# Carried state of the first three blocks joined in PSUM, and a new issue order, in a recurrence-and-mixer kernel

## The chip, the cores and the metric

The kernel runs on one core of one Trainium2 chip. Its engines are TensorE (PE; its weight loads are listed as PEld), VectorE (DVE), ScalarE (ACT), GpSimd (POOL) and SyncE (SP), which here only issues transfers. Each engine works through its own list of instructions in order; semaphores hold an instruction until what it needs is there. The metric is device time in microseconds of one execution; lower is better. "Before" is the median of three runs.

## The reference

A gated linear recurrence over 768 steps, for 4 batches and 8 heads of 48 channels, and behind it a mixer with two pairs of matrix products:

```python
for t in range(S):                       # per batch and head, S = 768
    state = alpha[t][:, None] * state + outer(k[t], v[t])     # 48 x 48
    y[t] = q[t] @ state
x = y of all heads side by side          # 768 x 384 per batch
h = relu(x.T @ w_tok1) @ w_tok2          # over the 768 positions, 256 hidden
u = x + h.T
out = u + relu(u @ w_ch1) @ w_ch2        # over 384 channels, 1536 hidden
```

Inputs and output are float32; the kernel's products are bfloat16 with float32 sums.

## The kernel before

**Blocks.** The 768 positions of a batch are cut into three blocks of 256, so there are twelve blocks, numbered 0 to 11; blocks 0 to 2 are batch 0. A block loads four tiles of 384 KB (alpha, k, q, v). With cumulative sums of the logarithms of alpha, made by PE from triangular matrices, keys and queries are scaled so that the recurrence becomes plain products: transposes of keys and queries, a key-query product in two halves ("G"), a causal mask on DVE that also copies it out of PSUM (L709), and a product with the values ("y") to which the part from the carried state is added ("ia", "ib"). Blocks 0 to 5 transpose keys and queries on PE; from block 6 on a transposing transfer does it, issued by SP.

**The carried state.** Each block makes key-value products in PSUM ("K", a pair of banks, one per half of the block). The state behind a half is (K + state before) times the decay of that half. The first state of a batch has no predecessor and is made by one multiplication out of PSUM (`sfirst`, L751). Every other state takes two steps: a sum out of PSUM into an SBUF tile `tmp` on DVE (`sadd`, L754), and a multiplication of `tmp` on DVE or POOL (`smul`, L757). The state is kept in bfloat16, 128 x 384.

**The mixer** of a batch follows its three blocks: token products (L791, L796), a sum (L800), a transposition (on PE for batches 0 and 1, L807), then 24 groups of the first channel product (L815), evacuated with a relu by ACT (L786) or DVE (L788), and six rows of the second (L820), evacuated by DVE (L824) and stored.

**What sets the order.** `build` only names the operations and the engines that may run them. The order of issue on every engine, the engine of each operation and the buffer of each value stand as written lists, `ORDER` and `BUFS`, in the source; `Plan.run` takes them as they are. In `ORDER`, `K1t` means operation K of block 1 on PE; the last letter is the engine: t PE, s ACT, v DVE, g POOL, y SP. A load's engine is the one that issues it, so `ld_vt0y` stands in SP's list and `ld_vt0s` would stand in ACT's list among its computations. All 64 input loads of the kernel before are issued by SP; three of the 25 stores are issued by ACT.

**Fillers.** `f1_` and `f3_` entries are one or three products of 512 columns on a tile of zeros (`fill`), written into a bank whose real content comes afterwards. Thirty such products are in the order before; twelve of them stand ahead of PE's first real work.

Keys, queries and alpha of blocks from 3 on are first multiplied pairwise (`P`, `k0a`, `q0r`; L578, L634, L638), since from there on two positions are joined to one; `scaled` (L642) then multiplies keys and queries by the exponentials. `copy` (L686 on ACT, L687 on DVE or POOL) makes casts, evacuations and moves.

Of the kernel before, what the change touches and what calls it, by code (L numbers as in the profile page):

```python
# [95 lines left out]
HD, DT, DCH = 384, 256, 1536  # L96
# [19 lines left out]
def build(g):  # L116
# [12 lines left out]
    def attention(n):  # L129
# [16 lines left out]
        la, E, IE = V("la"), V("E"), V("IE")  # L146
# [26 lines left out]
        wide = n in WIDE  # L173
# [196 lines left out]
mask0_1v P4g f1_G11t x1_0s E3s IE3s evk2v G1_1t sm1_1g trq2t ldw_wt20y mask1_1v lnP4s vs1_1g ib1t ldw_wt21y vb2s k0a3g  # L370
f3_K2t evq2s K2t f3_G02t y1_1t G0_2t cw_wt10s G1_2t ld_kt4y sa0_2v kk3v ia1t ldw_wc10y mask0_2v sm0_2g vs0_2g cw_wt11s
ldw_wc11y y0_1t t1_0_1_0t t1_0_1_1t t1_0_0_0t t1_0_0_1t ld_qt4y ka3g x0_1s ldw_wc12y kb3g ia2t ib2t ldw_wc13y x1_1s
mask1_2v t1_0_1_2t t1_0_0_2t y0_2t vs1_2s q0r3g t1_0_1_3t cw_wt20g t1_0_0_3t vb3s y1_2t x0_2v ldw_wc14y trk3t
ldw_wc15y t1_0_1_4t t1_0_0_4t x1_2v evk3v t1_0_0_5t qq3g t1_0_1_5t vs1_3s vs0_3s cum4t kc3s ht_0_1s ln14s ht_0_0v K3t
cw_wt21s r14s ld_at5y IE4s t2_0_2t E4s ld_vt4y ld_kt5y s0_3v u_0_2v t2_0_1t sa1_3v t2_0_0t t2_0_3t u_0_0v u_0_3v trq3t
t2_0_4t t2_0_5t up_0_1t u_0_1v up_0_0t k0a4g u_0_5v ldw_wc20y evq3s ld_qt5y ldw_wc21y cw_wc10g ut_0_1s kk4g u_0_4v
ut_0_0v G0_3t G1_3t mask1_3v cw_wc11s ldw_wc22y up_0_2t ib3t ka4g q0r4g qq4g c1_0_0_0t c1_0_2_0t ld_at6y y1_3t
c1_0_1_0t ut_0_2s rt_0_0_0v x1_3v mask0_3v rt_0_1_0s ldw_wc24y ldw_wc23y sm1_3g trk4t cw_wc12s c1_0_2_1t c1_0_3_1t
c1_0_0_1t c1_0_1_1t c1_0_4_1t rt_0_2_0v rt_0_3_1s rt_0_1_1v trq4t cw_wc13s rt_0_0_1s rt_0_2_1s cw_wc14g cw_wc15g
rt_0_4_1v c1_0_6_0t c1_0_7_1t ldw_wc25y evq4v c1_0_9_1t y0_3t rt_0_9_1v P5v evk4s rt_0_6_0s x0_3v c1_0_8_1t c1_0_7_0t  # L380
rt_0_7_1s kc4s c1_0_10_1t c1_0_11_1t vb4g kb4g lnP5s rt_0_7_0s k0a5g ln15s ld_vt5y rt_0_10_1v cum5t G1_4t mask1_4v
rt_0_11_1s r15s rt_0_8_1s G0_4t c1_0_4_0t c1_0_3_0t IE5s mask0_4v vs0_4g ld_at7y kk5v c1_0_10_0t c1_0_5_0t c1_0_5_1t
rt_0_4_0s cw_wc20s c1_0_8_0t q0r5v c1_0_9_0t c1_0_6_1t rt_0_3_0s E5s rt_0_8_0s rt_0_5_1s c1_0_11_0t rt_0_5_0s
rt_0_6_1s trk5t qq5v vs1_4v ia4t y0_4t cw_wc21g rt_0_11_0s K4t trq5t evk5v sa0_4v c2_0_1_0t rt_0_9_0s sm0_4v
rt_0_10_0v cw_wc24g sa1_4v P6v ld_at8y sm1_4v kc5v vb5g cw_wc22s c2_0_5_0t c2_0_2_0t evq5s x0_4s cw_wc23s cw_wc25s
lnP6s ld_kt6y c2_0_2_1t c2_0_5_1t t1_1_1_0t G1_5t G0_5t P7g vs1_5g t1_1_1_1t c2_0_1_1t c2_0_1_2t c2_0_5_2t ld_qt6y
c2_0_1_3t c2_0_5_3t vs0_5s mask0_5v ld_at9y ld_vt6y c2_0_2_2t mask1_5v cum6t o_0_1v o_0_5v K5t c2_0_2_3t ia5t y0_5t
ib4t sa0_5v ln16s sm0_5v o_0_2v lnP7s k0a6g y1_4t cum7t t1_1_1_2t t1_1_0_0t x1_4v ib5t E6s y1_5t t1_1_0_1t t1_1_0_2t
x0_5s c2_0_3_0t r16s ln18s t1_1_0_3t x1_5v t1_1_0_4t t1_1_1_3t t1_1_0_5t IE6s t1_1_1_4t q0r6v kk6v t1_1_1_5t c2_0_0_0t
st_0_5y ld_kt7y ht_1_0s ht_1_1s ld_qt7y st_0_1y c2_0_3_1t t2_1_5t vb6s t2_1_0t E7s u_1_5v t2_1_2t t2_1_3t t2_1_4t  # L390
t2_1_1t u_1_2v u_1_3v c2_0_0_1t c2_0_3_2t qq6g ln17s k0a7g c2_0_0_2t u_1_0v c2_0_4_0t up_1_1t u_1_4v c2_0_3_3t u_1_1v
up_1_0t IE7s P8g ut_1_1v dk6y up_1_2t ka6g kb6s ut_1_0s r17s vs0_6s c2_0_4_1t c2_0_0_3t ld_at10y ld_vt7y o_0_3v
ut_1_2v dq6y kk7g dk7y c1_1_10_1t c1_1_9_1t c1_1_1_1t rt_1_10_1v r18s rt_1_1_1s vs1_6g kc6g lnP8s c1_1_2_0t ld_qt8y
P10v o_0_0v K6t vb7s q0r7g c2_0_4_2t cum8t s0_6v sa1_6v P9g c1_1_2_1t c1_1_0_1t c1_1_10_0t c1_1_3_0t qq7g vs1_7g kb7s
ld_vt8y E8s lnP10s rt_1_0_1s rt_1_2_1v rt_1_10_0v ld_kt8y c1_1_4_1t ld_qt9y rt_1_2_0v rt_1_9_1v ka7s vs0_7s sm1_6v
c2_0_4_3t c1_1_7_0t ld_kt9y dq7y c1_1_11_0t ld_vt9y st_0_0y lnP9s IE8s c1_1_8_1t rt_1_4_1s o_0_4v kc7s rt_1_7_0s
c1_1_9_0t cum9t c1_1_11_1t c1_1_1_0t c1_1_0_0t rt_1_8_1s rt_1_11_1s rt_1_1_0s pq6s ln19s q0r8v rt_1_3_0v rt_1_11_0v
rt_1_9_0v c1_1_5_0t qq8g K7t c1_1_5_1t k0a8g rt_1_0_0v rt_1_5_0v c1_1_3_1t rt_1_3_1s rt_1_5_1s c1_1_6_1t c1_1_7_1t
sa0_7v c1_1_4_0t sm0_7v r19s rt_1_7_1s ld_kt10y dq8y sa1_7v c1_1_6_0t rt_1_6_1v IE9s G0_6t G1_6t rt_1_6_0s rt_1_4_0s
kk8g E9s vb8s ln110s vs1_8s pq7s q0r9g ld_qt10y mask0_6v c2_1_4_0t k0a9g c2_1_4_1t dk8y c2_1_1_0t mask1_6v kk9g ib6t  # L400
y0_6t x0_6v c2_1_4_2t c2_1_4_3t sm1_7g y1_6t c2_1_3_0t st_0_4y c1_1_8_0t o_1_4v st_0_2y G0_7t G1_7t vb9s vs0_8s
rt_1_8_0s mask0_7v c2_1_1_1t qq9g c2_1_3_1t pq8s c2_1_3_2t ia7t y0_7t cum10t r110s E10s mask1_7v k0a10v dk9y kc8s dq9y
c2_1_1_2t c2_1_0_0t c2_1_3_3t c2_1_1_3t q0r10v qq10g K8t o_1_3v x1_6v c2_1_0_1t ka9g sa0_8v ib7t o_1_1v sm0_8g IE10s
vs1_9s vs0_9s x0_7s y1_7t ia8t kb9s ld_at11y G0_8t x1_7s mask0_8v G1_8t t1_2_0_0t t1_2_0_1t t1_2_0_2t t1_2_1_0t kk10g
kc9s t1_2_1_1t t1_2_1_2t c2_1_0_2t st_1_1y ld_vt10y y0_8t t1_2_0_3t pq9g mask1_8v K9t t1_2_1_3t s0_9v x0_8s ib8t y1_8t
x1_8s t1_2_0_4t t1_2_1_4t c2_1_2_0t sa1_9v ln111s ka10g dq10y t1_2_0_5t t1_2_1_5t sm1_9g dk10y kb10g P11g ht_2_1s
r111s ht_2_0v lnP11s vb10s G1_9t G0_9t c2_1_2_1t t2_2_5t c2_1_0_3t mask1_9v ib9t ld_kt11y c2_1_2_2t y1_9t t2_2_3t
mask0_9v t2_2_4t u_2_5v u_2_3v cum11t t2_2_0t y0_9t u_2_4v ux_2_1y vs1_10s st_0_3y x1_9s c2_1_2_3t pq10g IE11s E11s
u_2_0v x0_9v o_1_2v c2_1_5_0t vs0_10g G0_10t t2_2_2t c2_1_5_1t c2_1_5_2t t2_2_1t c2_1_5_3t mask0_10v kc10v ia10t K10t
y0_10t c1_2_8_1t u_2_2v u_2_1v c1_2_3_1t c1_2_7_1t sa0_10v rt_2_3_1s rt_2_8_1v c1_2_5_1t rt_2_7_1s o_1_0v x0_10v  # L410
c1_2_4_1t c1_2_6_1t ld_qt11y rt_2_6_1s ux_2_0y ld_vt11y rt_2_4_1v c1_2_0_1t c1_2_2_1t k0a11g c1_2_1_1t kk11g q0r11g
rt_2_0_1s c1_2_5_0t c1_2_2_0t sm0_10g rt_2_5_1v qq11g sa1_10v rt_2_2_1s st_1_3y dk11y vb11g rt_2_1_1s dq11y kc11g
rt_2_2_0s st_1_4y c1_2_8_0t c1_2_9_0t c1_2_4_0t c1_2_3_0t c1_2_10_1t c1_2_9_1t rt_2_8_0v rt_2_5_0v o_1_5v vs1_11v
rt_2_4_0v sm1_10v vs0_11s rt_2_3_0s c1_2_11_0t rt_2_9_0s rt_2_9_1s c1_2_11_1t K11t rt_2_10_1s c1_2_0_0t rt_2_11_0v
pq11g c2_2_5_0t rt_2_0_0s c2_2_5_1t rt_2_11_1v sa0_11v G0_11t G1_11t G1_10t mask0_11v mask1_10v t1_3_1_0t mask1_11v
c2_2_5_2t st_1_0y c2_2_5_3t c2_2_3_0t c2_2_3_1t ib10t y1_10t t1_3_1_1t t1_3_1_2t c2_2_3_2t x1_10v ia11t y0_11t
t1_3_0_0t sm0_11g t1_3_0_1t x0_11s ib11t t1_3_1_3t y1_11t x1_11v o_2_5v t1_3_1_4t c2_2_3_3t o_2_3v t1_3_0_2t t1_3_0_3t
t1_3_0_4t t1_3_0_5t t1_3_1_5t st_2_5y st_1_2y ht_3_1v c1_2_6_0t c1_2_10_0t ht_3_0s c1_2_1_0t t2_3_0t u_3_0v t2_3_1t
# [460 lines left out]
```

## Time and profile before

| | |
|---|---|
| median of three runs | 166.98 us (165.88 to 167.26) |
| the profiled execution's own time | 167.16 us |
| its span | 165.5 us |
| instructions | 4049 |
| PE, DVE, ACT, POOL busy, share of the span | 93%, 69%, 60%, 47% |
| HBM read, written | 25.17 MB, 4.72 MB |
| share of the 16 DMA engines taken by the main queue | 78.9% |

Times are from the start of the span. "Busy" of PE is modelled from the start of each product, since products overlap in the array. A group line gives engine, operation, tiles, shapes and count; then busy time in us and the mean of one in ns; then the engine's idle time just before these instructions and what ended it. In a timeline the bracket holds the idle time and what ended it.

### The profile page before, as it was taken

How to read it: one execution, taken by the hardware profiler on the slowest of the kernel's cores; microseconds unless marked ns; L12 is line 12 of the kernel's file. 1: busy time of each engine (PE TensorE's matmuls, PEld its weight loads, DVE VectorE, ACT ScalarE, POOL GpSimd, SP SyncE). 2: the span in 40 equal slices, each digit the busy share in tenths (PEclk: the TensorE clock that was granted, in tenths of full speed). 3: DMA queues.
4: the chain of work that ended last, by engine and by line, in shares of the span. 5: the costliest groups of instructions: out<-in, count | busy, mean ns of one | idle time of the engine just before them, and what ended most of it. 6: DMA issues, size and time to landing. Idle time of an engine off the chain costs nothing.

```text
span 165.5 us, 4049 instructions
## 1 busy us (share of the span) xinstructions
PE 153.9 (93%) x1599; PEld 97.9 (59%) x1599; DVE 113.5 (69%) x200; ACT 98.7 (60%) x186; POOL 77.4 (47%) x87
## 2 busy tenths in 40 slices
PE   7849799799999999999999999999899999999992
PEld 2425657376667576665666676665566656566660
DVE  4059999698989987667776888985686703544232
ACT  3776699897999765589899965526502304162100
POOL 4055575899643344876689698397320000000000
PEclk9999999999999999999999999999999999999999
DMA  4999999999999799999999999889401362030114
GB/s 126 318 280 307 275 307 347 350 330 303 263 354 366 199 279 284 270 230 280 218 281 168 263 240 155 189 176 238 120 0 51 111 127 95 19 128 0 48 55 182
DMA packets 76322, 34.46 MB, mean 208 GB/s; under 512 B 68112, under 2 KB 76304, under 8 KB 76304
## 3 DMA queue, kind: packets, MB, share of 16 engines
q1 hardware_dynamic: 75872, 33.63, 78.9%
q10 hardware_dynamic: 432, 0.59, 1.0%
q8 instruction: 12, 0.20, 0.5%
q14 instruction: 6, 0.05, 0.1%
HBM read 25.17 MB, written 4.72 MB: 181 GB/s over the span
## 4 chain that ended last, share of the span: by engine, by line
PE 64%; DMA 13%; POOL 6%; SPq 4%; ACT 4%; issue 3%; DVE 2%; POOLq 0%; DVEq 0%
PE ps L820 26%; PE ps L815 20%; PE ps L593 9%; DMA in<-in_v_dram 6%; DMA in<-in_q_dram 5%; PE ps L791 4%; POOL pkq L642 3%; PE ps L796 3%; SPq L534 3%; DMA tpk<-pkq 3%; PE ps L655 1%; POOL in L638 1%; DVE pkk L642 1%; ACT vb L686 1%; PE ps L807 1%
## 5 line engine op out<-in xcount | busy, mean ns | idle before, releaser
L820 PE MATMUL ps<-wc,rt 128*128 128x384 bf16 (+2 forms) x300 | 53.2, 320 | 0.0
L815 PE MATMUL ps<-ut,wc 128*128 128x384 bf16 x288 | 50.9, 326 | 0.1
L786 ACT ACTIVATE rt<-ps 128x384 bf16<-128x384 f32 x59 | 26.9, 493 | 28.0 <-PE ps L815 27.7
L815 PEld LDWEIGHTS <-wc 128*128 128x128 bf16 x288 | 27.4, 98 | 17.7 <-issue 0.4
L820 PEld LDWEIGHTS <-rt 128*128 128x128 bf16 x300 | 27.6, 98 | 16.7
L709 DVE TENSOR_TENSOR gtm<-ps,mk 128x1024 bf16<-128x1024 f32 x24 | 28.5, 1219 | 4.6 <-PE ps L593 3.4
L788 DVE TENSOR_SCALAR rt<-ps 128x384 bf16<-128x384 f32 x37 | 19.4, 553 | 13.3 <-PE ps L815 13.2
L824 DVE TENSOR_TENSOR o<-ps,u 128x384 f32<-128x384 f32 (+2 forms) x25 | 13.1, 536 | 12.9 <-PE ps L820 12.9
L642 POOL TENSOR_TENSOR pkq<-in,E 128x768 bf16<-128x768 f32 x9 | 16.3, 1816 | 5.2 <-DVE in L638 3.3
L642 POOL TENSOR_TENSOR pkk<-in,IE 128x768 bf16<-128x768 f32 x7 | 12.7, 1817 | 9.4 <-ACT E L626 7.5
L686 ACT CAST vb<-in 64x384 bf16<-64x384 f32 (+1 forms) x22 | 14.1, 640 | 3.6 <-DMA in<-in_v_dram 2.3
L800 DVE TENSOR_TENSOR u<-ps,x 128x384 bf16<-128x384 f32 x24 | 12.1, 552 | 3.9 <-PE ps L796 3.6
L593 PE MATMUL ps<-zs 128*128 128x512 bf16 x30 | 9.7, 457 | 2.6 <-ACT IE L626 1.2
L791 PE MATMUL ps<-x,wt 128*128 128x384 bf16 x48 | 11.1, 326 | 0.0
L796 PE MATMUL ps<-ht,wt 128*128 128x384 bf16 x48 | 9.9, 327 | 0.8 <-POOL wt L687 0.8
L634 POOL TENSOR_TENSOR in<-in,in 128x384 f32<-128x384 f32 x8 | 8.0, 999 | 5.7 <-DVE pkk L687 2.6
L686 ACT CAST x<-ps 128x384 bf16<-128x384 f32 x12 | 5.5, 480 | 7.9 <-PE ps L593 7.8
L754 DVE TENSOR_TENSOR tmp<-ps,ss 128x384 f32<-128x384 f32 x16 | 8.8, 553 | 0.7 <-PE ps L593 0.3
L687 POOL CAST vb<-in 64x384 bf16<-64x384 f32 (+1 forms) x12 | 7.0, 581 | 4.8 <-DMA in<-in_v_dram 2.4
L593 PE MATMUL ps<-tpq,tpk 48*64 48x128 bf16 (+1 forms) x288 | 8.2, 219 | 0.8 <-POOL tpq L687 0.7
L757 POOL TENSOR_TENSOR ss<-tmp,E 128x384 bf16<-128x384 f32 x9 | 7.5, 834 | 3.0 <-PE ps L593 1.6
L593 PE MATMUL ps<-vb,gtm 128*128 128x48 bf16 x192 | 8.7, 184 | 0.0
(91 smaller groups left out, 208.2 us busy)
## 6 DMA issues: line engine op xcount, KB each, us to landing
in<-in_alpha_dram SPq DMA_DIRECT2D x12, 384.0 KB, 5.4
in<-in_q_dram SPq DMA_DIRECT2D x12, 384.0 KB, 5.6
in<-in_k_dram SPq DMA_DIRECT2D x12, 384.0 KB, 5.6
in<-in_v_dram SPq DMA_DIRECT2D x12, 384.0 KB, 5.5
in<-in_moe_w_ch_dram SPq DMA_DIRECT2D x12, 384.0 KB, 6.3
out_dram<-o SPq DMA_DIRECT2D x20, 192.0 KB, 2.4
in<-in_moe_w_tok_dram SPq DMA_DIRECT2D x4, 384.0 KB, 5.5
out_dram<-o ACTq DMA_DIRECT2D x3, 192.0 KB, 1.9
```

The costliest lines, as they stand in the source:

```text
L593: return self.pe.matmul(out, lhsT=lhsT, rhs=rhs, start=start, stop=stop, skip_group_check=True)
L642: self.shared(self.eng[e].tensor_tensor(self.t(dst)[:, :, :, 0:D], self.t(src).rearrange("p h s d -> p s h d"), bass.AP(tensor=f.tensor, o ...
L686: return self.act.copy(d, s)
L709: self.nc.vector.tensor_tensor(self.t(gtm)[:, hf, :, :], self.pair(gp).rearrange("p a (j t) -> p (a j) t", t=128), bass.AP(tensor=m.tensor ...
L786: self.act.activation(d, s, AF.Relu)
L788: self.nc.vector.tensor_scalar_max(d, s, 0.0)
L791: self.pe.matmul(self.bank(bank)[:, 0:HD], lhsT=self.wt1[:, kc, m * 128 : m * 128 + 128], rhs=self.t(x), start=(kc == 0), stop=(kc == NS - 1))
L796: self.pe.matmul(self.bank(bank)[:, 0:HD], lhsT=self.wt2[:, kc, i * 128 : i * 128 + 128], rhs=self.t(hts[kc]), start=(kc == 0), stop=(kc = ...
L800: self.nc.vector.tensor_tensor(self.t(u)[:, i % 3], self.bank(bank)[:, 0:HD], self.t(x), ALU.add)
L815: self.pe.matmul(self.bank(bank)[:, 0:HD], lhsT=self.wc1[:, kc, mc * 128 : mc * 128 + 128], rhs=self.t(ut)[:, 3 * half : 3 * half + 3, kc, ...
L820: self.pe.matmul(self.bank(bank)[:, 0 : cz - ca], lhsT=self.t(rts[mc][0])[:, i * 128 : i * 128 + 128], rhs=self.wc2[:, mc, ca:cz], start=( ...
L824: self.nc.vector.tensor_tensor(self.t(o)[:, ca:cz], self.bank(bank)[:, 0 : cz - ca], self.t(u)[:, i % 3, ca:cz], ALU.add)
```

## The change

For blocks 0 to 2, a state that has a predecessor is no longer summed on DVE. The predecessor (bfloat16, in SBUF) is multiplied with the identity on PE and added to the key-value products that lie in the PSUM bank; then one multiplication out of PSUM on DVE, the function that made first states, makes the new state. That holds for four states: the second half of block 0, both halves of block 1, and the first half of block 2. The names `sa` and `sm` stay, on PE and DVE in place of DVE and DVE or POOL. From block 3 on nothing changes in the computation.

```diff
         states = [before]
         for hf in range(nst):
             s_, sp = V("ss"), states[-1]
-            if sp is None:
+            if sp is not None and not turned:
+                ad = O(f"sa{hf}_", pe([384]), 10 + hf, writes=[kp], reads=[sp[0]], preds=[KO, sp[1]],
+                       emit=lambda e, hf=hf, s0=sp[0]: g.sjoin(kp, s0, hf))
+                so = O(f"sm{hf}_", dve(384), 11 + hf, writes=[s_], reads=[kp, E], preds=[ad, et],
+                       emit=lambda e, s_=s_, hf=hf: g.sfirst(s_, kp, E, hf, wide))
+            elif sp is None:
                 so = O(f"s{hf}_", dve(384), 10, writes=[s_], reads=[kp, E], preds=[KO, et],
...
+    def sjoin(self, kp, s0, hf):
+        self.mm(self.bank(kp, hf)[:, 0:HD], self.idn, self.t(s0), False, True)
```

The lists `ORDER` and `BUFS` are replaced as a whole. The head of the old and of the new order:

```diff
-ld_at0y f3_trq0t f3_cumw1t f3_cumw0t f3_G00t ln0s ld_at1y ld_at3y ld_qt0y f1_trk0t cumw0t ld_kt0y ln1s ld_vt0y E0s
-cumw1t ld_vt1y ld_kt1y Et0s ln13s qq0v IE0s ld_at2y IE1s E1s f3_K0t f1_K0t kk0g P3g trq0t trk0t vb0s K0t f1_G00t evq0v
...
+ld_at0y ln0s ld_kt0y ld_vt0s cumw0t ld_at1y ln1s E0s ld_at3s ld_qt0y qq0v ld_kt1y cumw1t IE0s kk0v ld_at2y IE1s kk1g
+trq0t Et0s vb0s f1_trk0t f1_K0t E1s ln2s K0t trk0t ld_qt2s ld_vt1y f1_G00t ld_qt1y f3_G00t Et1s s0_0v evq0v evk0s
+sa1_0t sm1_0v P3v f3_y0t G1_0t ln13s vb1s vs1_0g ld_kt2y G0_0t lnP3s mask1_0v cumw2t trk1t ld_kt3s K1t ldw_wt10s IE2s
```

What the new lists hold, counted against the old ones: 21 of the 64 loads are issued by ACT (ten of them ahead of the first L815 product of batch 0), and 11 of the 25 stores. Fillers are 18 products, none ahead of PE's first real work. Of the query scalings on DVE or POOL (`qq`), six are on POOL in place of nine, that of block 11 among those now on DVE. In the pair of steps that scale block 3's queries, `q0r3` is now on DVE and `qq3` stays on POOL; `cw_wt20`, a cast of a token weight, moves from POOL to DVE, and `cw_wt21` stays on ACT. `kk1` and `kk3` move from DVE to POOL and `kk0` from POOL to DVE; `evk0`, the copy of block 0's transposed keys, moves from DVE to ACT. The relu evacuations stand at 57 on ACT and 39 on DVE in place of 59 and 37; the evacuations of `x` at 18 and 6 in place of 12 and 12. The transfers that transpose stay on SP; `ld_vt11`, on SP ahead of the two transposes of block 11 before, is on ACT.

More of the change, by code (lines that the diff above doesn't have):

```diff
@@ L370 @@
[L370 to L404, printed above, removed]
@@ L415 @@
[L415 to L418, printed above, removed]
-c1_2_7_0t t2_3_2t st_2_3y u_3_1v t2_3_5t c2_2_4_0t rt_2_7_0v u_3_2v t2_3_3t rt_2_1_0s rt_2_6_0s c2_2_1_0t t2_3_4t
@@ new lines @@
+rt_3_10_1s rt_3_4_0v rt_3_9_1v c2_3_1_0t c2_3_2_0t c1_3_8_1t rt_3_9_0v c1_3_3_1t rt_3_1_1v rt_3_8_1v rt_3_3_1v
+rt_3_4_1s c2_3_4_0t c2_3_3_0t c2_3_1_1t c2_3_5_0t c2_3_0h1_0t c2_3_1_2t c2_3_3_1t st_2_0s rt_3_11_0s rt_3_10_0v
+c2_3_0h1_1t c2_3_0h1_2t c2_3_5_1t c2_3_0h1_3t c2_3_4_1t c2_3_1_3t c2_3_4_2t c2_3_4_3t c2_3_0h0_0t c2_3_2_1t c2_3_2_2t
+c2_3_3_2t o_3_1v o_3_0h1v st_2_1s c2_3_5_2t o_3_4v st_3_4s c2_3_2_3t c2_3_5_3t o_3_5v c2_3_3_3t c2_3_0h0_1t st_3_1y
+o_3_3v c2_3_0h0_2t o_3_2v st_3_5s st_3_0h1y c2_3_0h0_3t st_3_3y o_3_0h0v st_3_0h0y st_3_2s
```

81 lines of the change are left out of this document (57 added, 24 removed), and 22 rows, old and new, of the table BUFS.

## Prediction

> **What bounds the kernel now.** I read the page first, then busy time in chosen stretches, then the chain of waits through the places where the TensorE was not full.
>
> ```profile
> span 165.5 us, 4049 instructions
> PE 153.9 (93%) x1599; PEld 97.9 (59%) x1599; DVE 113.5 (69%) x200; ACT 98.7 (60%) x186; POOL 77.4 (47%) x87
> ```
>
> The share of PE is modelled and says little by itself. Stretches say more. The columns are: stretch, its length, busy time of PE, PEld, DVE, ACT and POOL with instructions begun, granted clock, DMA share, GB/s.
>
> ```profile
> 1.06:4.90 3.84, 3.84 (x10) 1.36 (x11) 1.83 (x17) 1.49 (x2) 1.59 (x7) 1.00 0.75 200
> 12.80:30.20 17.40, 15.22 (x246) 10.37 (x242) 17.25 (x23) 14.34 (x25) 9.93 (x14) 1.00 1.09 313
> 36.50:162.20 125.70, 124.58 (x1233) 79.60 (x1229) 86.71 (x147) 71.00 (x142) 56.66 (x56) 1.00 0.75 186
> ...
> sum 30.00, PE 23.93 PEld 15.60 DVE 22.83 ACT 24.33 POOL 17.27; mean PE 3.99 PEld 2.60 DVE 3.81 ACT 4.06 POOL 2.88
> ```
>
> The last line sums the six stretches from 5 to 35 us. The reader is to see three regimes. From 36.5 to 162.2 us PE is busy 124.58 of 125.70 us: there the kernel costs its matrix products and nothing else, and no product in that part is added or taken away. Before 36.5 us no engine rules alone: from 12.8 to 30.2 us DVE is busy 17.25 of 17.40 us, and the DMA share is 1.09, so the transfers are full too. ACT has 30.00 - 24.33 = 5.67 us free between 5 and 35 us. So the change can be worth what it does to the start of the long PE stretch, plus the few holes inside it (125.70 - 124.58 = 1.1 us by this view).
>
> How the start comes about is in the chain of waits (start, length, what):
>
> ```profile
> 21.99 7.64 DMA in<-in_q_dram
> ...
> 29.77 0.99 POOL in L638
> ...
> 30.76 0.82 POOL wt L687
> 31.59 1.79 POOL pkq L642
> ...
> 33.42 0.63 PE ps L655 x8
> ...
> 34.08 1.34 ACT tpq L686
> ...
> 35.45 0.62 PE ps L593 x16
> 36.08 0.44 PE ps L807 x6
> 36.52 0.17 PE ps L593 x4
> 36.69 0.33 PE ps L815 x2
> ```
>
> The queries of block 3 land at 29.63 us; POOL scales them, casts a weight piece in between, scales again; PE transposes, ACT copies out, and after products and a transposition the first channel product (L815) runs at 36.69 us. It is no matter of blocks 0 to 2 at all.
>
> **The change part by part.** The state, by groups:
>
> ```profile
> L754 DVE TENSOR_TENSOR tmp<-ps,ss 128x384 f32<-128x384 f32 x16 | 8.8, 553 | 0.7 <-PE ps L593 0.3
> L757 POOL TENSOR_TENSOR ss<-tmp,E 128x384 bf16<-128x384 f32 x9 | 7.5, 834 | 3.0 <-PE ps L593 1.6 <-DVE pkk L642 1.2
> L751 DVE TENSOR_TENSOR ss<-ps,E 128x384 bf16<-128x384 f32 x4 | 2.2, 550 | 0.4 <-PE ps L593 0.4
> L593 PE MATMUL ps<-la,u 128*128 128x384 bf16 x18 | 4.9, 325 | 0.5 <-ACT rt L786 0.3 <-ACT la L587 0.2
> ```
>
> Four sums of 0.553 us leave DVE (2.2 us), three of the four products after them leave POOL (2.5 us) and come to DVE at 0.550 (1.65 us). Four identity products of 384 columns come to PE; none stands in the trace, and the nearest row is L593 la,u, 0.325 us each to the end. One step of the state falls from 0.553 + 0.834 to 0.325 + 0.550 us, half a microsecond, four times. On the path to 36.69 us this is worth nothing directly, since that path runs through block 3. Off it, DVE's own list up to block 0's first token evacuation stays about as long (a weight cast, a query scaling and two multiplications of keys or alpha come to it, two key scalings and two copies out leave it). The join also adds a wait: an identity product stands in PE's queue until the state before it is made, with fillers, the other mask products and the next block's transposes behind it. In the start PE has idle time for that: the two rows below are idle times of 1.54 and 1.05 us. If the cover went, it would cost at most a step's 0.55 us four times.
>
> ```profile
> 12.13 0.62 PE L655 MATMUL ps<-idn,pkk 128*128 128x128 bf16 x8 [1.54 <-POOL pkk L642]
> 18.86 0.62 PE L655 MATMUL ps<-idn,pkq 128*128 128x128 bf16 x8 [1.05 <-POOL pkq L642]
> ```
>
> *Order at the start.* In the new order the query scaling of block 3 (0.99 us on POOL) is on DVE, where the same form takes about the L751 time, 0.55, and the weight cast (0.82 us) is no longer between it and POOL's second scaling. With the landing where it is, the chain shortens by 0.44 + 0.82 = 1.26 us. But the copy on ACT at 34.08 us has its own predecessors, and these do not move: the second piece of the second token weight is cast there first.
>
> ```profile
> 31.88 0.83 ACT L686 CAST wt<-in 128x768 bf16<-128x768 f32 x1 [0.56 <-DMA in<-in_moe_w_tok_dram]
> ```
>
> In both orders a logarithm-sized operation and two exponentials of some 0.45 us follow before the copy; from 32.7 that is 33.9 to 34.1 us, so with this landing only 0.2 us are won. In the new order that piece is issued on ACT ahead of the loads for block 4, so it may land about one transfer sooner. The ends are thus 0.2 and 1.26 us earlier; I take 0.9, nearer the chain that the profile names.
>
> *Loads on ACT.* Ten loads move to ACT's queue before the first channel product, and some twenty in all. What an issue costs there:
>
> ```profile
> 0.81 2.39 SPq L534 DMA_DIRECT2D in<-in_alpha_dram  x3
> 3.24 1.15 SPq L534 DMA_DIRECT2D in<-in_q_dram  x1
> ...
> L534 SPq DMA_DIRECT2D in<-in_alpha_dram x5: 455/1077/1262, 0.8 to 15.2; - x5
> ...
> L574 ACTq DMA_DIRECT2D out_dram<-o x3: 338/377/444, 156.6 to 161.0; - x3
> ```
>
> The third and fourth rows give shortest, median and longest ns. An issue is 0.455 us when the queue is empty and 1.1 us behind others; ACT's few stores at the end took 0.377. With 0.46 the ten cost 4.6 us. Counted by the two orders up to the third copy of the transposed mixer input, ACT also loses three casts of 0.83 us and gains one copy out of PSUM; three operations of some half a microsecond leave and three come.
>
> ```profile
> L686 ACT COPY tpk<-ps 128x1024 bf16<-128x1024 bf16 x1 | 1.0, 1023 | 0.0
> ```
>
> That is 3 x 0.83 - 1.02 = 1.5 us less. So 3.1 us must fit into its 5.67 free ones, and they do, with 2.6 us over. I cost the loads at nothing; the cover is gone when an issue takes over (5.67 + 1.5)/10 = 0.72 us.
>
> By the Trainium skill (DMA: Bandwidth & Descriptors, "Issuing engines are not separate DMA queues") DMAs from any engine run on the same 16 engines and interleave, and a second issuing engine saves only issue time. The share of 1.09 agrees; by that rule nothing lands sooner, which is the second rival below.
>
> *Fillers.* Before, 30 products of 512 columns on zeros keep PE occupied; afterwards 18, none of them ahead of the first real work. The first stretch above shows ten starts in 3.84 us, 0.43 us each; later three take 0.66 us until the next group, 0.22 each:
>
> ```profile
> 24.20 0.82 PE L593 MATMUL ps<-zs 128*128 128x512 bf16 x3
> 24.86 0.36 PE L593 MATMUL ps<-vb,gtm 128*128 128x48 bf16 x8
> ```
>
> So PE begins at half rate although the granted clock reads 1.00, and the fillers took that phase. Now the first cumulative products (four of 384 columns for each of two blocks) will. Eight products of 384 columns take about 8 x 0.16 = 1.3 us more so (384/512 of the 0.22 us at full rate is 0.16), among waits for loads; I cost it at nothing, at most 1.3.
>
> *Block 11.* The one clear hole in the long stretch:
>
> ```profile
> 111.89 1.81 POOL L642 TENSOR_TENSOR pkq<-in,E 128x768 bf16<-128x768 f32 x1
> 113.73 1.23 SPq L666 DMA_TRANSPOSE tpk<-pkq  x1
> 118.71 1.32 POOL L687 COPY tpq<-tpk 128x1024 bf16<-128x1024 bf16 x1 [2.57 <-DMA tpk<-pkq]
> 120.09 0.86 PE L593 MATMUL ps<-tpq,tpk 48*64 48x128 bf16 x48 [0.67 <-POOL tpq L687]
> L642 DVE TENSOR_TENSOR pkq<-in,E 128x768 bf16<-128x768 f32 x3 | 2.9, 956 | 5.7 <-DMA in<-in_q_dram 5.6
> ```
>
> POOL's 1.81 us scaling releases the transposing transfer, then POOL's copy, then PE, 0.67 us late. The new order gives the scaling to DVE (0.956), and block 11's values load on ACT's queue rather than ahead of the transposes on SP. It stands 0.85 us earlier, the hole closes: -0.7. The transfer could land no sooner behind other traffic: then 0.
>
> *All else* (eight more stores on ACT, evacuations dealt out anew among ACT and DVE, which are busy 71.00 and 86.71 us of the 125.70) lies beside a full PE: 0, between -0.4 and some +4 us.
>
> **Sum.** 167.16 us for the profiled execution (span 165.5 and 1.66 around it) - 0.9 - 0.7 = 165.6. The median of the runs shown is 166.98, so 0.8% under it. One per cent, 1.67 us, is about what a measurement of this kernel can tell from no change; the main case lies from 164.0 to 166.6.
>
> **Rivals.**
> *Holes close beyond that.* ACT and PE in the middle:
>
> ```profile
> 75.00:80.00 5.00, 4.56 (x32) 2.55 (x30) 4.31 (x9) 4.25 (x11) 3.19 (x3) 1.00 1.07 276
> ```
>
> 0.44 us is idle there, behind a knot of ACT work that the new order spreads; with the full 1.26 at the start it gives 167.16 - 1.26 - 0.7 - 0.44 = 164.8, and with an earlier landing of one load (1.1 us) 163.7. Take 164.2. Against: every order leaves knots of its own.
>
> *Transfers rule.* The same bytes through full queues: the last needed weight lands at 31.88 as now, 0.2 gained, block 11 waits for its transfer: 167.0. For it: the share of 1.09; against: the chain through POOL.
>
> *The change is slow to wake PE.* With half rate reaching into blocks 0 and 1, 1.3 us and a like sum for transposes, half covered: 165.6 + 1.3 = 166.9. By the Trainium skill (TensorE: Matmul & The Clock Gate, "What's actually happening") the array leaves half rate only after some 3.4 us of sustained work; the ten slow starts agree, and the figure says nothing about scattered work.
>
> *ACT's queue blocks* (slower). If a load on ACT waits for room as SP's do, at 1.15 us, ten cost 11.5 us; less 1.5 and the free 5.67 leaves 4.3 us on the path to the first channel product: 167.16 + 4.3 - 0.7 = 170.8. It decides from 0.72 us an issue on. For it: SP's median 1.077, and ACT waits in order, so a load held for a buffer holds the evacuations behind it. Against: only a third load in a row was slow at the start, and ACT's stand apart.
>
> *New holes* (slower). The order of every engine is new over 125 us that are now full to 1.1 us; three or four holes like block 11's put 3 us on: 168.9 and more.
>
> **How the numbers follow.** Main case 0.36 (somewhat over a third of it under 165.3), closing holes 0.17, transfers 0.08, waking 0.04, ACT's queue 0.20, new holes 0.15. Faster by over 1% (under 165.3): 0.13 + 0.17 = 0.30. Slower by over 1% (over 168.65): 0.20 + 0.15 = 0.35. Within: 0.23 + 0.08 + 0.04 = 0.35. The range reaches from 163.6 to 170.8 and leaves out some 0.04 below and, of the last two rivals, the worse halves. That the join does not take place is no case of its own: 16 sums would still stand on DVE, at the same time within 0.5 us.
>
> **What would show it.** The first L815 group before 36 us; rows of identity products on the state of 0.33 us and 12 sums left at L754; ACT's load issues near 0.46 us (wrong if near 1.1, with idle DVE and PE behind them); no wait of PE for the query copy of block 11; PE busy over 124 us in the 125 before its last product. I am wrong if the first L815 comes after 37 us or PE's waits for ACT grow by microseconds.

## The result and the profile after

The changed kernel takes 168.53 us in the median of four executions against 166.43 us for the kernel before on the same chip; the ratio is 1.011, with a 95% interval of 1.0062 to 1.0158. Beside later kernels it was run once more, at 1.0158 (1.009 to 1.0227). It is slower by a little over one per cent, and the forecast said 0.8% faster. Ratios and intervals, here and below, are of undisturbed executions alone, while medians are of all; in three runs below (the new run of the changed kernel, the join in the old order, and the first kernel with both the load on SP and zero products at the front) the profiled execution was a disturbed one, and of their traces only one wait of the first is used.

The profiled execution of the changed kernel took 167.97 us. The head of its page, with the granted clock in 40 slices:

```profile
span 166.3 us, 4027 instructions
PE 153.1 (92%) x1591; PEld 98.4 (59%) x1591; DVE 118.1 (71%) x205; ACT 96.3 (58%) x185; POOL 67.9 (41%) x79
PEclk9999995999999999999999999999999999999998
```

There is something new in the third line: in the seventh slice, 25 to 29 us, TensorE had half its clock. In the kernel before all forty slices read 9.

The stretches of the changed kernel (stretch, length, busy time of PE, PEld, DVE, ACT, POOL, granted clock, DMA share, GB/s), from two questions:

```profile
20.00:25.00 5.00, 2.96 (x49) 2.25 (x47) 3.24 (x4) 2.55 (x6) 2.28 (x3) 1.00 1.14 338
25.00:30.00 5.00, 5.00 (x80) 3.75 (x78) 3.51 (x5) 3.85 (x7) 4.08 (x5) 0.66 1.10 359
...
38.10:162.90 124.80, 124.56 (x1233) 79.52 (x1232) 92.05 (x152) 69.57 (x142) 48.67 (x51) 1.00 0.71 175
```

PE is busy 2.96 of the 5 us from 20 us on, then 5.00 of 5, but at a mean clock of 0.66. The long stretch is fuller than before: 0.24 us of it are idle (124.80 - 124.56) in place of 1.12. The first kind of its channel products, with the first and the last start, by the view of that line:

```profile
L822 PE MATMUL ps<-ut,wc x288: 322/326/337, 38.1 to 151.9; 128*128 128x384 bf16 x144
```

It starts at 38.08 us against 36.52 us in the timeline of the kernel before (36.69 us is where the chain of waits comes to it): 1.56 us later. From there to the start of the kernel's last product it is 124.58 us (38.08 to 162.66) against 125.36 us (36.52 to 161.88): 0.78 us shorter. 1.56 - 0.78 = 0.78 us is the difference of the two profiled executions (167.97 - 167.16 = 0.81). The ratio of 1.011 is more than that, 1.8 us; the hybrid orders below bear on why.

What ends at 38.10 us, in the chain of waits of the changed kernel (start, length, what):

```profile
21.30 1.43 SPq L560
22.73 0.05 issue
22.78 8.86 DMA in<-in_k_dram
31.64 0.02 issue
31.66 0.37 ACTq L560
32.03 0.04 issue
32.07 0.52 ACT pkk L690
32.59 0.05 issue
32.64 0.79 PE ps L597 x14
33.43 1.01 PE ps L803 x6
...
38.10 0.95 PE ps L822 x5
```

The chain no longer runs through block 3's queries. SP's load of block 4's keys lands at 31.64 us; 0.02 us later **ACT issues a load** (`ldw_wc15`, a piece of an output weight), and only then comes ACT's copy `pkk` of block 3's keys, for which the key-value products wait. Block 4's keys are used by neither the copy nor the issued load. The landings in the trace raise eight semaphores in turn, whichever engine issued the load; the record of this load's instruction names the semaphore that it waits for, and it is the one that block 4's keys raised last. ACT's list stands at the load until then. So a wait for a transfer of SP's stands in ACT's list, and ACT's computations behind it. The timeline has the same, and an earlier stall (start, length, what, and in brackets the idle time before and what ended it):

```profile
22.78 0.86 SPq L538 DMA_DIRECT2D in<-in_k_dram  x1
24.60 0.50 PE L597 MATMUL ps<-vb,pkk 64*128 64x96 bf16 x8 [1.99 <-POOL vb L691]
28.16 0.73 PE L798 MATMUL ps<-x,wt 128*128 128x384 bf16 x2
31.66 0.37 ACTq L560 DMA_DIRECT2D in<-in_moe_w_ch_dram  x1
32.64 0.34 PE L597 MATMUL ps<-vb,pkk 128*128 128x96 bf16 x4 [0.92 <-ACT pkk L690]
```

At 24.60 us PE has waited 1.99 us for POOL's cast of block 2's values. The half clock follows that stall. Two causes offered themselves, then: ACT held by a load's wait, and stalls of PE with what they do to the clock.

### The profile page after: what moved, and what is told of

Read it like the earlier page. It is cut to its first block, busy times and chain, and to the rows that moved or that the text cites. A ratio compares the mean times of both kernels' runs of the same rounds, so it can differ in the third digit from the quotient of the medians.

```text
span 166.3 us, 4027 instructions
## 1 busy us (share of the span) xinstructions
PE 153.1 (92%) x1591; PEld 98.4 (59%) x1591; DVE 118.1 (71%) x205; ACT 96.3 (58%) x185; POOL 67.9 (41%) x79
## 4 chain that ended last, share of the span: by engine, by line
PE 79%; DMA 8%; DVE 6%; SPq 3%; ACT 1%; issue 1%; ACTq 0%; DVEq 0%
PE ps L822 28%; PE ps L827 27%; PE ps L597 13%; DMA in<-in_k_dram 5%; PE ps L803 4%; PE ps L798 4%; DMA in<-in_alpha_dram 3%; DVE gtm L713 2%; PE ps L659 2%; PE ps L814 1%; DVE u L807 1%; SPq L560 1%; SPq L538 1%; DVE pkk L646 1%; SPq L554 1%
## 5 line engine op out<-in xcount | busy, mean ns | idle before, releaser
L827 PE MATMUL ps<-wc,rt 128*128 128x384 bf16 (+2 forms) x300 | 54.1, 320 | 0.0
L793 ACT ACTIVATE rt<-ps 128x384 bf16<-128x384 f32 x57 | 25.8, 489 | 23.8 <-PE ps L822 21.9
L795 DVE TENSOR_SCALAR rt<-ps 128x384 bf16<-128x384 f32 x39 | 20.2, 552 | 11.0 <-PE ps L822 9.8
L690 ACT CAST x<-ps 128x384 bf16<-128x384 f32 x18 | 8.6, 479 | 10.1 <-PE ps L597 8.6
L646 POOL TENSOR_TENSOR pkq<-in,E 128x768 bf16<-128x768 f32 x6 | 10.9, 1815 | 7.7 <-DVE wt L691 3.0
L597 PE MATMUL ps<-la,u 128*128 128x384 bf16 x18 | 5.8, 388 | 6.0 <-ACT la L591 6.0
L798 PE MATMUL ps<-x,wt 128*128 128x384 bf16 x48 | 11.1, 331 | 0.0
L646 DVE TENSOR_TENSOR pkq<-in,E 128x768 bf16<-128x768 f32 x6 | 5.7, 955 | 6.1 <-ACT E L630 5.0
L582 POOL TENSOR_TENSOR in<-in 128x384 f32<-128x384 f32 x6 | 6.0, 999 | 8.0 <-DVE wc L691 3.9
L597 PEld LDWEIGHTS <-gtm 128*128 128x128 bf16 x192 | 7.9, 98 | 2.3 <-issue 1.0
L691 POOL CAST vb<-in 64x384 bf16<-64x384 f32 (+1 forms) x10 | 5.3, 533 | 7.9 <-ACT vb L690 5.3
```

The lines of the kernel that those rows point to most:

```text
L597: return self.pe.matmul(out, lhsT=lhsT, rhs=rhs, start=start, stop=stop, skip_group_check=True)
L646: self.shared(self.eng[e].tensor_tensor(self.t(dst)[:, :, :, 0:D], self.t(src).rearrange("p h s d -> p s h d"), bass.AP(tensor=f.tensor, o ...
L690: return self.act.copy(d, s)
L793: self.act.activation(d, s, AF.Relu)
L795: self.nc.vector.tensor_scalar_max(d, s, 0.0)
L798: self.pe.matmul(self.bank(bank)[:, 0:HD], lhsT=self.wt1[:, kc, m * 128 : m * 128 + 128], rhs=self.t(x), start=(kc == 0), stop=(kc == NS - 1))
```

## Experiments

**The two parts of the change, apart.** The join in the old order, and the new order without the join.

```diff
 (old order, join: sa on PE, sm on VectorE directly behind it)
-sa1_0v
+sa1_0t sm1_0v
...
 (new order, no join)
-sa1_0t sm1_0v
+sa1_0v sm1_0v
```

One of the four states is shown; the other three are changed alike.

> The kernel before, with its order, and only the join: four sums on PE instead of DVE, the multiplication behind each out of PSUM on DVE right behind it. If the loss comes from the new order: same time as before within 0.5% (0.997 to 1.003), first L815/L822 product at 36.0 to 36.9 us. Rival 'the join itself costs' (PE holds its queue for the state before): PE waits of 0.3 us or more in front of identity products and a first channel product at 37.5 us or later, ratio 1.008 or more.

> The changed kernel, with its order, but the old computation of the state: the four sums on DVE, the multiplications on DVE behind them. Theory 'new order': the stall at block 2's products and the late start stay, ratio 1.009 to 1.016, with up to 0.5 us more since DVE does 1.9 us more work in a stretch in which it is full only up to 23.5 us. Rival 'the join costs': ratio falls to 1.003 or less.

Measured: the join in the old order 167.41 us, ratio 1.0056 (1.0034 to 1.0078); the new order without the join 169.99 us, 1.0185 (1.0126 to 1.0244). The first lies between the two ranges that were expected, the second above its range. So most of the loss is the order's, not the join's. The join costs half a per cent in the old order; in the new order it is worth some 0.7% by the midpoints (1.0185 against 1.011), with intervals that overlap and on two chips. Without it PE waits longer, for POOL's copy of values of block 0, and POOL's copy has waited 1.31 us for the state's multiplication on DVE. In the source that multiplication (`smul`) goes through `shared`, which makes such operations of DVE and POOL follow each other in order of issue; the join's multiplication (`sfirst`) does not.

```profile
19.89 0.32 PE L592 MATMUL ps<-vb,gtm 128*128 128x48 bf16 x4 [2.33 <-POOL vb L686]
```

**Block 2's values earlier.** Loaded ahead of block 4's alpha, and cast on POOL ahead of block 4's pairwise product.

```diff
-ld_kt2y ... ld_at4y ... ld_vt2y ... P4g ... vb2g
+ld_kt2y ld_vt2y ... ld_at4y ... vb2g P4g ...
```

> The changed kernel, with the load of block 2's values issued ahead of block 4's alpha, and POOL's cast of them ahead of POOL's product for block 4. Theory 'late values' (PE stood 2.0 us at block 2's key-value products because these values landed at 23.6 us, behind loads that ACT had issued): the values land near 21 us, that wait falls under 0.5 us, the granted clock between 25 and 30 us stays at 1.00, the first L822 product comes at 36.5 to 37.0 us instead of 38.1, and the kernel at 0.995 to 1.003 of the kernel before. Rival 'ACT is held' (an issue on ACT waits for a load of SP): the wait before K of block 3 at 31.4 us stays at about 1 us, the first L822 product comes no more than 0.5 us sooner, ratio 1.007 to 1.011. Rival 'cold start': no difference over 0.3 us, ratio 1.011.

Measured: 168.57 us, 1.0108 (1.0072 to 1.0143): no gain. The stall at 24.6 us goes and the first x product (L798) stands at 25.3 us in place of 28.2, but PE then waits before block 3's keys, and runs at half rate after it:

```profile
28.23 0.62 PE L659 MATMUL ps<-idn,pkk 128*128 128x128 bf16 x8 [1.53 <-POOL pkk L646]
...
29.31 1.13 PE L798 MATMUL ps<-x,wt 128*128 128x384 bf16 x3
```

Three products of 384 columns take 1.13 us here, some 0.32 us from one start to the next, against 0.16 at full rate. The first channel product stays at 38.12 us, as the rival "ACT is held" had it: the stall was beside the chain that ended last, and ACT's wait (1.55 us idle before the copy) still ended it.

**The output weight's load off ACT, or later on ACT.** In the first kernel SP issues it; in the second it stays on ACT, behind the two casts it held.

```diff
-cw_wt20v ldw_wc15s kc3s
+cw_wt20v ldw_wc15y kc3s
...
-ldw_wc15s kc3s t1_0_1_5t ht_0_0v K3t cum4t ht_0_1s qq3g
+kc3s t1_0_1_5t ht_0_0v K3t cum4t ht_0_1s ldw_wc15s qq3g
```

> The changed kernel, with one load, the last piece of the first channel weight, issued by SP instead of ACT at the same place of the order. Theory 'ACT is held': ACT's move of block 3's keys comes at about 31.2 instead of 32.07 us, PE's wait before block 3's products falls from 0.9 to about 0, the first L822 product comes about 0.9 us sooner (37.2 us), ratio about 1.005. Theory 'late values': the stall of 2.0 us at 22 to 24.6 us stays as it is, and of the 1.6 us by which the first L822 product is late at least 0.7 stay. If only the late values mattered, the first L822 product would stay at 38.1 us.

> The changed kernel with one move on ScalarE's queue: the load of the sixth output-weight tile is issued behind the scaled-key cast and the first hidden-state cast (ht) instead of ahead of them; it stays on ScalarE. Theory 'ScalarE is held by the load's wait': the casts no longer stand behind a wait that ended only when a transfer of SyncE's queue landed, so the time comes out as in the run that gave this load to SyncE, whose first y product stood at 37.2 us and whose ratio was 1.0035: first y product at 37.0 to 37.4 us, 167.2 to 167.6 us. Rival 'SyncE's queue': what helped there was the changed order of SyncE's issues and landings; then the first y product stays at 38.1 us and the time at 168.4 to 168.6 us.

Measured: on SP 167.41 us, 1.0035 (1.000 to 1.007); later on ACT 167.35 us, 1.0076 (1.0034 to 1.0119). In neither trace does PE wait before block 3's key-value products. ACT's copy and these products in the second:

```profile
29.85 0.50 ACT L690 COPY pkk<-pkk 64x384 bf16<-64x384 bf16 x1
30.41 0.34 PE L597 MATMUL ps<-vb,pkk 128*128 128x96 bf16 x4
```

The first channel product stands at 37.2 and 36.7 us in place of 38.1, as the wait's theory said, though the two profiled executions are not quite of one kind with the changed kernel's. Both have a whole clock (1.00), where most of the others of the same kernels read 0.979 to 0.990. In the first the whole start ran some 2.7 us later (the identity product of block 1's second half at 20.24 us in place of 17.54), so that the stall at 24.6 us could not arise; in the second that stall was 1.25 us. By times the first is decided: beside it on the same chip stands the kernel with block 2's values first, which keeps the load at its old place, at 1.0108 (1.0072 to 1.0143). The times of the second were run on another chip, and its interval reaches that of the changed kernel, so by times alone it is not decided; the kernels with zero products in the stall, below, decide it.

**Zero products put back at the front.** Nine of them, where PE stands still until 5.2 us; then the same with the load on SP, and then with block 2's values first as well.

```diff
-ld_at0y ln0s
+ld_at0y f3_trq0t f3_cumw1t f3_cumw0t ln0s
```

> The changed kernel with nine zero products of the kernel before put back ahead of the first cumulative product, where TensorE otherwise stands still until 5.2 us. Theory 'cold start': the products between 5.2 and 11 us, spaced 0.32 us apart in the changed kernel, run at 0.16 us, block 0's gate arrives some 0.5 us earlier and about half of that or more reaches the first y product: 37.4 to 37.8 us, 167.8 to 168.2 us. Rival 'the start is covered': loads land in turn at 1.2 us apart, and the phase ends with what the late loads and ScalarE allow; then the first y product stays within 0.2 us of 38.1 and the time within 0.3 us of 168.5.

> Both edits at once: the sixth output-weight tile loaded by SyncE (0.9 us by its own run) and the nine zero products at the front. If each cost is a term of its own: 166.6 to 167.2 us, first y product at 36.4 to 36.9 us. If the start is covered: 167.2 to 167.6 us, as with SyncE's load alone, first y product at 37.2 us. If the earlier start only lets TensorE run into the wait for block 2's values (2.2 us in the changed kernel, not seen in the run with SyncE's load): a hole of 1 us or more stands before block 2's key-value products again, and the time is 167.4 us or more.

> The two edits and the third, block 2's values loaded ahead of block 4's gate inputs and cast ahead of block 4's mask product on GpSimd. Alone this third edit changed the time by nothing (1.0108) because the hole came back before block 3's keys. Theory 'ScalarE and the start were the bound': with them gone the values count, first y product at 36.0 to 36.5 us and 166.0 to 166.6 us. Rival 'holes wander': the wait comes back elsewhere between 20 and 32 us and the time is that of the two edits, or longer.

Measured: 169.68 us, 1.0185 (1.009 to 1.028); 167.0 us, 1.0063 (1.0017 to 1.011); 166.6 us, 1.004 (1.0004 to 1.0075). The first came out worse than both of its theories, with the first channel product at 39.5 us. The cold start is not shown to cost this change anything. With the zero products ahead of them the first real products still run at half rate, but the second group, block 1's, runs at full rate, where the changed kernel still has half rate (its row last):

```profile
3.59 1.49 PE L597 MATMUL ps<-zs 128*128 128x512 bf16 x3
5.15 1.12 PE L597 MATMUL ps<-la,u 128*128 128x384 bf16 x3
7.59 0.65 PE L597 MATMUL ps<-la,u 128*128 128x384 bf16 x3 [0.77 <-ACT la L591]
...
7.63 1.12 PE L597 MATMUL ps<-la,u 128*128 128x384 bf16 x3 [0.74 <-ACT la L591]
```

So the half rate does end sooner, but the groups start when ACT has made the logarithms of alpha, at 5.2 and 7.6 us with the zero products or without, and what they win there is not in the time. The first kernel stalls for ACT's copy later, longer than the changed one did:

```profile
32.93 0.34 PE L597 MATMUL ps<-vb,pkk 128*128 128x96 bf16 x4 [2.15 <-ACT pkk L690]
```

The second is no faster than the load on SP alone (1.0035, on another chip). What the third gains over the second, 0.2%, is within their intervals. Its time reaches the range of the first theory of its expectation (166.0 to 166.6 us), but not by that theory: its first channel product stands at 37.3 us and not at 36.0 to 36.5, behind a stall of 1.53 us before block 3's keys, at half rate again, as the rival "holes wander" had it.

**Keeping PE busy through the stall.** Seven zero products in the stall before block 2's key-value products; alone, and with the load behind ACT's casts. A third kernel has the late load, block 2's values first, and the seven zero products in the stall that this leaves before block 3's keys. The changed kernel was run beside them.

```diff
-E3s IE3s K2t
+E3s IE3s f3_K2t f1_K2t f3_y1t K2t
...
-y0_2t ... trk3t
+y0_2t ... f3_trk3t f1_trk3t f3_y2t trk3t
```

> The changed kernel once more, unaltered, so that the runs beside it share a chip with it: 168.0 to 169.0 us, ratio 1.007 to 1.016, mean granted clock 0.986 to 0.990, first y product at 37.9 to 38.3 us.

> The changed kernel with seven zero products ahead of block 2's key-value products, in the hole of 2.2 us in which TensorE waits for block 2's values. They end before the values come, so no product of the kernel is later. Theory 'the hole lowers the clock': no half-rate products follow at 25 to 28 us, the mean granted clock comes back to 0.996 or above in nearly all executions, and the first x products come 0.5 to 1.2 us earlier; as ScalarE's scaled-key cast still ends at 32.6 us the first y product gains only 0.2 to 0.6 us: 167.9 to 168.3 us. Rival 'the clock is no matter of the hole': clock 0.987 again and 168.5 us. Third: if ScalarE's wait alone binds, the clock is whole and the time is still 168.5 us.

> The same seven zero products, and the load of the sixth output-weight tile issued behind ScalarE's two casts (alone 1.0076 and a clock of 0.986 to 0.99 in most executions). If the two costs add up: clock 0.996 or above, first y product at 36.4 to 36.8 us, 166.3 to 166.9 us, ratio 1.000 to 1.004. If the clock is no matter of the hole: as without the zero products, 167.3 us or ratio 1.007.

> The late load, block 2's values loaded and cast first (its hole gone, but one of 1.7 us then stands before block 3's keys), and seven zero products in that hole. If all three costs of the new order are then paid back and its gain in the long stretch (0.8 us) stays: clock 0.996 or above, first y product at 35.8 to 36.4 us, 165.4 to 166.2 us, ratio 0.994 to 1.000. Rival 'the landings rule the first phase': first y product at 36.7 us or later and a ratio of 1.003 or more, whatever is warm.

Measured, on one chip: the changed kernel 169.1 us, 1.0158 (1.009 to 1.0227); zero products alone 169.15 us, 1.0185 (1.012 to 1.025); with the late load 166.48 us, 1.0039 (1.0007 to 1.0072); with the values first too 166.38 us, 1.0029 (0.9995 to 1.0063).

No theory had the zero products alone right: the half rate at 25 us goes, PE is earlier, and runs into ACT's wait that much harder. The timeline of that kernel:

```profile
31.58 0.37 ACTq L560 DMA_DIRECT2D in<-in_moe_w_ch_dram  x1
31.99 0.51 ACT L690 COPY pkk<-pkk 64x384 bf16<-64x384 bf16 x1 [2.00 <-DMA in<-in_k_dram]
32.56 0.34 PE L597 MATMUL ps<-vb,pkk 128*128 128x96 bf16 x4 [1.99 <-ACT pkk L690]
...
33.41 2.72 PE L803 MATMUL ps<-ht,wt 128*128 128x384 bf16 x8
```

ACT's idle time ahead of the copy is 2.00 us, PE's is 1.99, and now the half clock comes after this stall: eight products of 384 columns in 2.72 us, 0.32 us apart. The window says so too:

```profile
33.40:37.60 4.20, 4.20 (x34) 2.59 (x32) 2.73 (x7) 2.37 (x5) 4.12 (x5) 0.65 1.12 341
```

So ACT's wait hid the stall: with the stall removed alone, the wait stalls PE for 2 us in its place and halves its clock for some 3 us more. With the load late as well (timeline of the kernel with the late load and the zero products):

```profile
29.99 0.51 ACT L690 COPY pkk<-pkk 64x384 bf16<-64x384 bf16 x1
30.55 0.34 PE L597 MATMUL ps<-vb,pkk 128*128 128x96 bf16 x4
31.68 0.38 ACTq L560 DMA_DIRECT2D in<-in_moe_w_ch_dram  x1
32.09 0.83 ACT L690 CAST wt<-in 128x768 bf16<-128x768 f32 x1 [0.91 <-DMA in<-in_k_dram]
32.98 0.50 PE L803 MATMUL ps<-ht,wt 128*128 128x384 bf16 x2 [0.38 <-ACT wt L690]
```

The copy is made at 29.99 us, two microseconds sooner, and the wait, still there, holds a later cast for 0.91 us and PE for 0.38. By the chain of waits the first channel product, at 36.4 us, still comes behind that cast. The granted clock, 0.979 to 0.990 in the eight executions of the changed kernel, is 0.997 to 1.000 in all ten of this one, and in all ten of the next. The time comes back from 1.0158 to 1.0039, as the expectation "the two costs add up" had it; the next, at 1.0029 with its first channel product at 36.6 us, lies between its two theories.

The wait's share is shown: the kernel with zero products alone and this one differ by the place of one load, on one chip, and stand at 1.0185 (1.012 to 1.025) and 1.0039 (1.0007 to 1.0072). The share of the stall and of the lowered clock is not. Among the executions of the late load alone, three with a clock of 0.997 or more took 166.6 to 167.1 us (166.86 in the middle), and the other six that its ratio counts 167.45 us in the median; that makes some 0.6 us, as an estimate. But between kernels it does not show: with the late load, zero products or none are 1.0039 against 1.0076 on two chips; the load on SP alone gave 1.0035 with a clock of 0.986 to 0.990 in eight of ten executions, and the kernel with SP's load, zero products at the front and the values first 1.004 with 0.976 to 0.990 in all ten.

**What is left of the gain.** The old order for its first 302 entries (up to block 4's key-value products) and the new one from there; and the old order for 612 entries, so that of the change only block 11's part and what follows it is left.

```diff
 ORDER:
-the new order from its first entry
+302 (or 612) entries of the old order, then the new order's remaining entries
 (state sums of blocks 0 to 2 on VectorE; 15, or 8, values in another buffer of their kind)
```

> The order of the kernel before up to and with the key-value products of block 4 (302 entries, state sums on VectorE, all loads on SyncE there), and from there the new order; a dozen values take another buffer of their kind so that lifetimes do not meet. If the first phase is the whole loss and the long stretch's gain of 0.8 us (the closed hole of block 11 and a shorter stall near 76 us) is real: ratio 0.995 to 0.997, first y product within 0.3 us of the kernel before. If the gain lies beside the path that ends last, or comes only with the new first phase: ratio 0.999 to 1.003. If the seam makes holes of its own: above 1.003, with holes right behind 50 us.

> The order of the kernel before for 612 entries (to some 100 us), and from there the new order: of the change only block 11's part (its query scaling on VectorE, its value load on ScalarE, the stores) is left. If the hole of block 11 was worth its 0.7 us: ratio 0.995 to 0.997 and no TensorE wait for block 11's transposed queries. If the wait goes and the time stays, it was made up for later: ratio 0.999 to 1.002.

Measured: 167.29 us, 1.0058 (1.0031 to 1.0085), and 166.2 us, 1.0009 (0.9982 to 1.0035). The first has a hole behind its seam:

```profile
53.11 0.83 ACT L686 CAST wc<-in 128x768 bf16<-128x768 f32 x1 [2.02 <-DMA in<-in_moe_w_ch_dram]
...
53.66 1.14 PE L823 MATMUL ps<-wc,rt 128*128 128x384 bf16 x6 [1.99 <-DVE tmp L757]
```

It is not of the kind of the changed kernel's: ACT waits for the weight that it casts, and PE for DVE's sum of a state. So this hybrid says little on the gain. The second has no such hole, and block 11's queries come in time:

```profile
117.57 0.65 PE L823 MATMUL ps<-wc,rt 128*128 128x384 bf16 x3
118.15 0.86 PE L593 MATMUL ps<-tpq,tpk 48*64 48x128 bf16 x48
```

There is no wait in brackets where the kernel before had 0.67 us. Still the stretch from the first channel product to the last product is 125.36 us long, the same as before, and the time is the same. In the ten profiles used here that have the new order from start to end, this stretch was between 124.5 and 125.3 us: 0.1 to 0.9 us shorter. Of the kernel before there is one profile, so how far its own stretch varies is not known.

Both hybrids also show something about the kernel before. Their first 302 entries are its own, and their first channel products stand at 34.9 and 35.1 us, 1.6 and 1.4 us ahead of the profiled execution that the forecast started from. A difference shows where transfers were slower in that execution (a window of the second hybrid, and from its timeline the wait for block 0's keys):

```profile
10.00:15.00 5.00, 4.40 (x70) 2.56 (x69) 3.82 (x6) 4.79 (x9) 2.98 (x3) 1.00 1.17 325
```

```profile
11.57 0.62 PE L655 MATMUL ps<-idn,pkk 128*128 128x128 bf16 x8 [0.43 <-POOL pkk L642]
```

The profiled execution of the kernel before had waited 1.54 us at this place, and its transfers in these 5 us went at 273 GB/s:

```profile
10.00:15.00 5.00, 3.38 (x47) 1.90 (x49) 3.52 (x5) 3.37 (x7) 3.27 (x3) 1.00 1.03 273
```

Its 167.16 us lie above the medians of the kernel before beside all these runs (165.86 to 166.59 us). No version that was run is shown to beat the kernel before.

## Why the prediction was wrong, step by step

**The start, -0.9 us: wrong, +1.56.** In the sum the whole miss stands here, since the other term, -0.7, has -0.78 beside it in the profile. The step that failed is "I cost the loads at nothing". Its sizes held: ten issues of 0.37 to 0.59 us, near the 0.46 assumed and under the 0.72 at which the cover goes. By type, in the changed kernel (shortest, median, longest ns):

```profile
L538 ACTq DMA_DIRECT2D in<-in_q_dram x4: 374/374/374, 11.6 to 80.3; - x4
L538 ACTq DMA_DIRECT2D in<-in_k_dram x4: 374/374/375, 14.7 to 102.2; - x4
```

What it left out is that a load in an in-order list waits before it is issued, and that the wait is not for its own data. The step went by the length of an issue and had no term for the wait ahead of it: 0.94 us of ACT and 0.92 us of PE in the changed kernel, 2.00 and 1.99 us where PE came sooner. The slower rival "ACT's queue blocks" was right that ACT's computations stand behind a load, and named a load held for a buffer; it was wrong about how: not 1.15 us for every issue but 0.9 to 2.2 us once, at the load whose semaphore an SP transfer still held. Its time, 170.8, was too high for that reason. The other part of the step held: block 3's queries did land sooner, issued by ACT at 20.31 us and 7.4 us under way, so at 27.7 us against 29.63, and their chain stopped being the last. What came last in its place, ACT's copy of block 3's keys, the forecast did not look at.

**PE waiting for block 0 to 2's data: not priced.** "In the start PE has idle time for that" took idle time as free. Here it was not always free: four stalls of 1.99 to 2.33 us were each followed by half rate. The rival "slow to wake PE" came near to it, but it was put at the very start, on the missing fillers, where nine zero products gave nothing back.

**The fillers, 0 to 1.3: 0 at the front,** as taken; and in the stall they change the clock: with the load late on ACT, zero products there go with a whole clock in every execution. What that is worth in time is not settled.

**The join, nothing on the path: its sizes held.** Four identity products of 0.331 us (0.325 was assumed), 12 sums left:

```profile
L761 DVE TENSOR_TENSOR tmp<-ps,ss 128x384 f32<-128x384 f32 x12 | 6.6, 554 | 1.6 <-DVE ss L755 0.5 <-PE ps L597 0.4 <-POOL ss L764 0.4
L597 PE MATMUL ps<-ss,idn 128*128 128x384 bf16 x4 | 1.3, 331 | 0.3 <-DVE ss L755 0.3
```

PE waited 0.3 us for a state, all told. Its worth did not come out as nothing: in the old order it costs half a per cent, in the new one it seems to gain a little more than that.

**Block 11, -0.7 us: the mechanism right, the gain not shown to be its own.** The scaling went to DVE, POOL's copy came at 117.5 us, and PE no longer waits:

```profile
112.76 0.96 DVE L646 TENSOR_TENSOR pkq<-in,E 128x768 bf16<-128x768 f32 x1
113.79 1.24 SPq L670 DMA_TRANSPOSE tpk<-pkq  x1
117.46 1.34 POOL L691 COPY tpq<-tpk 128x1024 bf16<-128x1024 bf16 x1 [0.26 <-DMA tpk<-pkq]
120.38 0.86 PE L597 MATMUL ps<-tpq,tpk 48*64 48x128 bf16 x48
```

In the changed kernel's profile the long stretch is 0.78 us shorter, close to the forecast. But done alone (the hybrid of 612 entries, 0.9982 to 1.0035) it gains 0.3 us at best, and there the stretch has its old length although the hole is closed; so the agreement of 0.78 with 0.7 may be luck. Where the hybrid lost what the hole gave, no run here singles out.

**The sum's own start.** It was made against an execution of 167.16 us whose first phase was about 1.4 us behind that of the same order in two other executions. So a part of the chain it shortened may have been that execution's, not the kernel's. It was known that the three times given reached from 165.88 to 167.26; the forecast should have asked which of its waits the faster ones can have had.

The point "I am wrong if the first L815 comes after 37 us or PE's waits for ACT grow by microseconds" came true in its first half, at 38.08 us.

## What to carry to other kernels

A load given to a computing engine is a wait in that engine's list: ask which semaphore it counts on and whose transfer held that last, and put it behind the computations that something waits for. Where several engines take turns in a start, remove first the stall that the chain of waits names: removing the other alone gave nothing back here and made this one longer. Count the clock too, since after a stall of 2 us eight products stood 0.32 us apart in place of 0.16, which is 1.3 us. And read the first phase from more than one execution, since it differed by 1.4 us between executions of the same first phase.

## What the hardware showed

**Half rate after a stall of about 2 us, in a sparse stretch.** In four of these profiles (the changed kernel, the new order without the join, nine zero products at the front, seven in the stall) TensorE stalled for 1.99 to 2.33 us (idle times in brackets) between 17 and 33 us, and in each the granted clock of the following slices fell, to 0.65 and 0.66 in the two windows shown. A stall of 1.25 us (the kernel with the late load, at 24.4 us) left it whole; at 1.5 us it came both ways: half rate after 1.53 us before block 3's keys in the two kernels with block 2's values first, and none after 1.53 us at the same place in the order without the join, 1.52 us before block 2's key-value products with zero products at the front, and 1.54 us in the kernel before. And the stall of 1.99 us in the first hybrid at 53.7 us, with a full TensorE before it, left all forty slices at 9 in that execution. The Trainium skill (TensorE: Matmul & The Clock Gate, "HAM oscillation — how this bites in real kernels") has the mechanism, and gives gaps over some 3.4 us as the rule. Here shorter ones were enough where the work around them was sparse; that sparseness is the reason is argued, not shown.

**A granted clock of 1.00 beside half-rate products.** At the start, 5 to 10 us, products of 384 columns stand 0.32 us apart in the changed kernel while the column reads 1.00. With nine zero products from 1.06 us on it is so at 5.15 us and no longer at 7.59 us (0.16 us apart).

**Transfers issued by two engines share their semaphores.** The kernel's source names no semaphore; they are given out when the program is built. In five of the six traces with the load at its old place on ACT (the new run of the changed kernel among them) it was issued 0.02 to 0.03 us after block 4's keys landed: 31.66 after 31.64, 31.58 after 31.55, 31.67 after 31.65, 31.95 after 31.93, and 33.32 after 33.30. In the sixth, without the join, its semaphore had last been raised at 30.65 us by another load, ACT came to it at 32.64 us, and there was no wait.
